# FNet and GeGLU on one Trainium2 core: an eighth pass of the sequence DFT as seven block products, with its preparations moved ahead

## The chip, the cores and the metric

The kernel runs on one core of a Trainium2 chip. Its engines work side by side, each on its own instructions in the order in which the program gives them: TensorE (PE) multiplies, VectorE (DVE) and ScalarE (ACT) work element by element, GpSimd (POOL) helps, and SyncE (SP) issues the transfers between the device's memory and the core. An instruction that waits holds up everything behind it on its own engine; this holds for SP's transfers too. The metric is the device time of one execution in microseconds (us), as the median of several runs.

## The reference

```python
def _A_ref(x, dft_seq_re, dft_seq_im, dft_hid_re, dft_hid_im):
    a = jnp.einsum("bsd,ed->bse", x, dft_hid_re)
    b = jnp.einsum("bsd,ed->bse", x, dft_hid_im)
    y = jnp.einsum("ts,bse->bte", dft_seq_re, a) - jnp.einsum("ts,bse->bte", dft_seq_im, b)
    return y

def _B_ref(x, w_gate, w_up, w_down):
    g = jnp.einsum("bsd,df->bsf", x, w_gate)
    u = jnp.einsum("bsd,df->bsf", x, w_up)
    h = _gelu(g) * u
    return jnp.einsum("bsf,fd->bsd", h, w_down)
...
h = x + _A_ref(_layernorm(x, axis=-1), A_dft_seq_re, A_dft_seq_im, A_dft_hid_re, A_dft_hid_im)
h2 = h + _B_ref(_layernorm(h, axis=-1), B_w_gate, B_w_up, B_w_down)
```

x has 2048 rows of 448 columns. It is normed, the real part of its Fourier transform over the sequence and over the hidden dimension is formed as two products with cosine and sine matrices, and x is added. The sum h is normed and goes through a feed-forward part: a gate and an up product (448 by 1792 each), GELU of the gate times the up part, and a down product back to 448 columns, added to h.

## The kernel before

**Number format.** Every operand of a product is split into two fp16 halves, *hi* (the rounded value) and *lo* (what rounding left), and a product is three terms: hi by hi, hi by lo, lo by hi. ACT makes hi (L108), DVE makes lo (L112 or L114) out of the fp32 value and hi; so each split is a hand-over from ACT to DVE.

**Stages.** First comes the sequence DFT, the product of the 2048 x 2048 cosine and sine matrices (parts 0 and 1) with the normed x; its output comes in eight groups of 256 rows, called p = 0 to 7, each of two halves g. Behind each p comes its hidden DFT (`hid_mm`, 21 matmuls for each g). Then follow the gate and up products and the down product; the profile's lines L1039 and L1243 are theirs.

**Steps.** The sequence DFT is written as 64 steps (`N_STEPS`). Steps 0 to 15 take the 16 tiles of x as they come and fill eight accumulators (p = 0 and 1); `x_load`, `x_stats`, `x_hi`, `x_lo` prepare tile n + 2 or n + 3 in step n. From step 16 on, a pass is four steps, and two passes (part 0, part 1) make one p. A normal step is 24 matmuls of 448 columns and needs one weight tile `wr` split into `ws`. From step `FAST` = 36 on, a pass is computed as seven block products instead of eight (Strassen's scheme): 42 matmuls of 224 columns a step. It needs sums of weight blocks, made for each step by `fast_sums` (DVE), `fast_raw` and `fast_split` (ACT hi, DVE lo), together called the unit of a step, and sums of x tiles, called T0 to T7, which are made once: `t_load` reads two x tiles again (`tx`), `t_norm` norms them on ACT, `t_sums` adds them in four DVE instructions, `t_hi` and `t_lo` split them. T j is used in the step of a pass with j = 2 (n mod 4) + i, so T6 and T7 in its last step. The result of a fast pass, `zs`, is also split into hi and lo.

**What sets the order.** The order is written out by hand. `early[n]` holds work that is issued at the start of step n, `after[(n, half)]` work that is issued behind the first or second half of step n's matmuls. What stands earlier in the program comes earlier on every engine that it uses.

**Work that is slotted in.** `Weights(f, k)` loads a chunk f of the gate and up weights into `gu_raw` (two DMAs), `sums` adds blocks of it on DVE, `split(True)` splits the raw blocks, `split(False)` splits the sums, one step after another. `gu_raw` shares two buffers with `wh_raw`, the raw tiles of the hidden DFT's matrix: a load into one waits until the tile before in that buffer has been split. The first chunks, 13 and 11, follow wh_raw1 and wh_raw2. `hid_seed` (ACT, L712) writes x into the accumulator of a hidden DFT, of which there is one for all, and `hid_out` (ACT, L720 to L722) reads it when `hid_mm` is done; the seed for g = 1 thus stands behind the reading of g = 0. The layernorm of the feed-forward part (`ffn_norm_act`, `ffn_sums`, `ffn_split`) is also spread over the steps. The rings have 3 buffers for x tiles, 5 for `wr`, 6 for `ws`, and 7 PSUM banks for sums of the sequence DFT.

```python
fast_at = [FAST + n for n in (-4, -2, -1)] + list(range(FAST + 1, N_STEPS - 2))
```

Of the kernel before, what the change touches and what calls it, by code (L numbers as in the profile page):

```python
# [32 lines left out]
def kernel(  # L33
# [76 lines left out]
    def lo_part(dst, src, hi, scale=1.0):  # L110
        if isinstance(scale, float) and scale == 1.0:
            V.tensor_sub(dst, src, hi)  # L112
        else:
            V.scalar_tensor_tensor(dst, src, scale, hi, op0=ALU.mult, op1=ALU.subtract)  # L114
# [301 lines left out]
    N_STEPS = NT + 8 * (NP - 2)  # L416
# [32 lines left out]

    FAST = N_STEPS - 28
    A_RAW = ("A12", "A11", "A22")
    FORMS = ("S3", "S1", "S2", "S4")
    T_OPS = ("T1", "T3", "T4", "T2")
    PRODUCTS = ("A11", "B11"), ("A12", "B21"), ("S2", "T2"), ("S3", "T3"), ("S1", "T1"), ("S4", "B22"), ("A22", "T4")
    fast_w, fast_s, fast_t, fast_acc, fast_e = {}, {}, {}, {}, {}

    def fast_views(n):
        raw = wr[n].rearrange("p (i b t) -> p i b t", i=2, b=4)  # L460
# [5 lines left out]
    def fast_sums(n):  # L466
        fast_s[n] = dft.tile([P, 8 * P], F32, tag="wr", bufs=5, name=f"sums{n}")
        fast_w[n] = [fast_tile(n, k, **place) for k, place in enumerate(fast_places(n))]
        raw, s, src, dst = fast_views(n)
        by_block = raw.rearrange("p i b t -> p b i t")  # L470
        V.tensor_add(s[:, 0:2], by_block[:, 1:3], by_block[:, 3:4].to_broadcast([P, 2, 2, P]))  # L471
        V.tensor_add(s[:, 2], s[:, 1], raw[:, :, 1])
        V.tensor_add(s[:, 3], raw[:, :, 0], s[:, 2])
# [56 lines left out]
    def fast_halves(n):  # L530
        p, part, qq = step_of(n)
        hi, lo = [zs[p][:, :, l, part * D : (part + 1) * D] for l in range(2)]
        src = fast_e[n][:, 0 : 2 * D].rearrange("p (g d) -> p g d", g=2)
        hi_part(hi, src)
        lo_part(lo, src, hi)

    def fast_out(n, k):

# [207 lines left out]


    gu, gw = {}, {}
    DFT_F = ((13, 14, 0), (11, 16, 1), (9, 18, 0), (7, 20, 1), (5, 22, 0), (3, 24, 1), (0, 28, 0), (1, 32, 0))
    JIT_F = range(2, 13, 2)  # L750

    early, after = {}, {}
# [10 lines left out]
        nc.sync.dma_start(gw[f], w_dram[f])  # L763

    for i, (f, n, k) in enumerate(DFT_F):
        ahead = 4 if i < 2 or n - DFT_F[i - 2][1] > 4 else 3
        at(after, (n - ahead, 0), lambda f=f, k=k: gu.update({f: Weights(f, k)}))
        at(early, n, lambda f=f: gu[f].sums())
        at(early, n + 1, lambda f=f: gu[f].split(True))
        at(early, n + 2, lambda f=f: gu[f].split(False))  # L770
        at(after, (n + 3, 0), lambda f=f: gu[f].store())
# [6 lines left out]
    for p, (n, half) in enumerate(turns):  # L778
        b, j = divmod(p, 2)
        m = (19, 24, 29, 36, 44, 52, 60)[p]  # L780
        last = ((20, 0), (25, 0), (30, 0), (38, 0), (48, 0), (56, 0), (61, 1))[p]
        m1 = last[0] + 1
        at(early, m - 4, lambda b=b, j=j: h_tile(b, j))
        at(early, m - 2, lambda p=p: hid_seed(p, 0))
        for g in range(2):

            place = last if g else (m, 0)
            at(after, place, lambda p=p, g=g: hid_mm(p, g), lambda p=p, g=g: hid_out(p, g))
            if g == 0:
                at(after, (m, 0), lambda p=p: hid_seed(p, 1))  # L790
        at(after, (n, half), lambda p=p: z_turn(p))
        at(early, m1 + p // 3 if p < 5 else N_STEPS - 7 + p, lambda b=b, j=j: ffn_rstd(b, j))
        at(after, (m1, 0), lambda b=b, j=j: h_store(b, j))
        if b < 2:

            m += 4 if p == 3 else 0
            at(early, m + 2, lambda b=b, j=j: ffn_bias(b, j), lambda b=b, j=j: ffn_norm_act(b, j, hp[b, j]))
            at(early, m + 3, lambda b=b, j=j: ffn_sums(b, j))
            at(early, m + 4, lambda b=b, j=j: ffn_split(b, j))
            for k in range(4):  # L800
                at(after, (m + 5 + k // 2, k % 2), lambda b=b, j=j, k=k: ffn_transpose(b, j, (k,)))
# [1 line left out]
    at(early, N_STEPS - 2, lambda: h_tile(NB - 1, 1))  # L803
    at(early, N_STEPS - 1, gelu_table)
    at(after, (N_STEPS - 2, 0), lambda: down_load(0), lambda: down_load(1))
    for j, n in ((0, 17), (1, 20), (4, 23), (5, 26), (6, 29), (2, 31), (3, 34), (7, 37)):
        at(after, (n - 2, 1), lambda j=j: t_load(j))
        at(early, n, lambda j=j: t_norm(j), lambda j=j: t_sums(j))
        at(after, (n, 0), lambda j=j: t_hi(j))
        at(after, (n, 1), lambda j=j: t_lo(j))  # L810
# [38 lines left out]
    for n in range(N_STEPS):  # L849
        if n == 0:  # L850
            for key in first:
                seq_acc(*key, last=key == first[-1])
        elif n >= FAST and n % 4 == 0:
            fast_begin(n)
        elif n >= NT and n % 4 == 0:
            for g in range(2):
                seq_acc(*step_of(n)[:2], g)
        if n + 3 < NT:
            x_load(n + 3)
        if n + 3 < FAST:  # L860
            seq_load(n + 5)

        if 0 < n < FAST - 3:
            seq_hi(n + 3)
        if 0 < n < NT - 2:
            x_rstd(n + 2)
            x_hi(n + 2)
            x_norm(n + 2)
        if 0 < n < NT - 3:
            x_stats(n + 3)  # L870
        if n == 0:
            seq_lo(2)
        if n + 3 < FAST:
            seq_lo(n + 3)
        if n in fast_at:
            unit = fast_at.index(n) + FAST
            fast_sums(unit)

            if n < FAST or n % 4 < 3:
                fast_raw(unit)  # L880
                fast_split(unit)
                if unit + 2 < N_STEPS:
                    seq_load(unit + 2)
        if n == 0:
            x_stats(3)
            x_lo(2)
        if 0 < n < NT - 2:
            x_lo(n + 2)
        for what in early.get(n, ()):
            what()  # L890
        if n >= FAST:

            last = n % 4 == 3
            one = [(i, k) for k in range(7) for i in range(2)] if last else [(i, k) for i in range(2) for k in range(7)]
            if n % 4 == 0 and n > FAST:

                one = [(i, k) for i in range(2) for k in range(5)] + [(i, k) for i in range(2) for k in (5, 6)]
            for m, (i, k) in enumerate(one):  # L900
                fast_mm(n, i, k)
                if last and i == 1 and k in (0, 2, 4, 6):
                    fast_out(n, k)
                    if n < N_STEPS - 1:
                        unit = n + 2
                        if k == 2:
                            fast_raw(unit)
                        elif k == 4:
                            fast_split(unit)
                            if unit + 2 < N_STEPS:  # L910
                                seq_load(unit + 2)
                if m in (6, 13):
                    for what in after.get((n, m // 7), ()):
                        what()
            continue

        if n < NT:
            one = [(key, n - n % 2 + key[0], 2 * (2 * key[1] + key[2]) + n % 2, n) for key in first]
            if n == 0:

                order = [(0, m) for m in (0, 2, 1)] + [(1, m) for m in range(3)]
                one = [(*a, (m,)) for jj, m in order for a in one[4 * jj : 4 * jj + 4]]
            elif n < 6:
                one = [(*a, (m,)) for m in (0, 2, 1) for a in one]
            else:
                one = [(*a, range(3)) for a in one]
        else:
            p, part, qq = step_of(n)
            one = [
                ((p, part, g), n, 4 * i + 2 * g + c, 4 * qq + 2 * i + c, range(3))  # L930
                for i in range(2)
                for g in range(2)
                for c in range(2)
            ]
            if qq == 3:

                one.sort(key=lambda a: a[0])
        for half in range(2):
            for key, unit, block, c, terms in one[half * len(one) // 2 : (half + 1) * len(one) // 2]:
                seq_mm(key, ws[unit], block, c, terms)  # L940
                if c == NT - 1 and 2 in terms and (n < NT or block in (5, 7)):
                    z_out(*key)
            for what in after.get((n, half), ()):
                what()
    z_turn(NP - 1)
    down_sums(0)
    gu[JIT_F[1]] = Weights(JIT_F[1], JIT_F[1] % 3)
# [331 lines left out]
    for q, t0, step, when in ((2, 5, 3, AT_A), (3, 14, 6, AT_B)):  # L1279
# [22 lines left out]
    right.close()  # L1302
    ps_ff = {
        tag: ctx.enter_context(tc.tile_pool(name=f"ps_{tag}", bufs=1, space=bass.MemoryType.PSUM, reuse_waits="tile"))
        for tag in ("Y", "X", "a0", "a1", "a2", "a3", "Z")
    }
    ps_ff["tr"] = ps_tr

# [11 lines left out]
    for t in range(NF):  # L1320
        w = gu.get(t + 2) if t + 2 in JIT_F else None
        n = PREP_AT.get(t)
# [258 lines left out]
```

## Time and profile before

| what | value |
|---|---|
| median of 3 runs | 701.72 us (701.16 to 701.92) |
| profiled execution, its own time | 701.11 us |
| its span | 699.3 us, 13800 instructions |
| PE busy | 694.1 us, 99% of the span |
| DVE busy | 556.3 us, 80% |
| ACT busy | 402.1 us, 57% |
| POOL busy | 106.7 us, 15% |
| granted TensorE clock | 1.00 |
| moved by DMA | 160.40 MB, mean 229 GB/s |

Busy time is counted in the profiled execution; its own time is longer than its span by 1.8 us, which lie around the span. The span starts with the first instruction. Rows of a timeline give start, duration, engine, line, operation, output and inputs by their names, shapes, a count, and in brackets the idle time before it with what ended it.

### The profile page before, as it was taken

How to read it: one execution, taken by the hardware profiler on the slowest of the kernel's cores; microseconds unless marked ns; L12 is line 12 of the kernel's file. 1: busy time of each engine (PE TensorE's matmuls, PEld its weight loads, DVE VectorE, ACT ScalarE, POOL GpSimd, SP SyncE). 2: the span in 40 equal slices, each digit the busy share in tenths (PEclk: the TensorE clock that was granted, in tenths of full speed). 3: DMA queues.
4: the chain of work that ended last, by engine and by line, in shares of the span. 5: the costliest groups of instructions: out<-in, count | busy, mean ns of one | idle time of the engine just before them, and what ended most of it. 6: DMA issues, size and time to landing. Idle time of an engine off the chain costs nothing.

```text
span 699.3 us, 13800 instructions
## 1 busy us (share of the span) xinstructions
PE 694.1 (99%) x5236; PEld 506.9 (72%) x5236; DVE 556.3 (80%) x1150; ACT 402.1 (57%) x789; POOL 106.7 (15%) x127
## 2 busy tenths in 40 slices
PE   8999999999999999999999999999999999999998
PEld 5555555555579888997644444469999999999997
DVE  7998766865899999985548798786777867899786
ACT  5877566675585556554427666655555453655631
POOL 0000000000001001000303333521120211232224
PEclk9999999999999999999999999999999999999999
DMA  8788888999876477374766878797879995877612
GB/s 276 244 238 284 242 290 215 328 279 294 221 216 166 122 196 199 124 210 174 148 226 230 284 241 251 191 334 234 216 227 331 243 302 174 321 277 273 231 42 80
DMA packets 116179, 160.40 MB, mean 229 GB/s; under 512 B 61968, under 2 KB 80528, under 8 KB 116112
## 3 DMA queue, kind: packets, MB, share of 16 engines
q1 hardware_dynamic: 116112, 159.51, 74.5%
q8 instruction: 41, 0.67, 0.4%
q14 instruction: 26, 0.21, 0.1%
HBM read 111.25 MB, written 34.34 MB: 208 GB/s over the span
## 4 chain that ended last, share of the span: by engine, by line
PE 94%; DVE 2%; ACT 2%; issue 1%; DMA 0%; POOL 0%; DVEq 0%; ACTq 0%; POOLq 0%
PE acc L645 20%; PE acc_f L521 16%; PE acc_d L1243 15%; PE pY L1039 15%; PE pZ L1039 10%; PE pX L1039 10%; PE y L731 9%; DVE gu_w L114 0%; ACT ws L108 0%; DMA x<-in_x_dram 0%; DVE ws L114 0%; DVE xs L112 0%; ACT y L722 0%; ACT hx L720 0%; ACT dn_w L108 0%
## 5 line engine op out<-in xcount | busy, mean ns | idle before, releaser
L1039 PEld LDWEIGHTS <-gw 128*128 128x128 f16 x1404 | 137.1, 98 | 47.0
L645 PE MATMUL acc<-xs,ws 128*128 128x448 f16 x864 | 164.7, 352 | 0.5 <-DVE xs L149 0.5
L645 PEld LDWEIGHTS <-ws 128*128 128x128 f16 x864 | 84.5, 98 | 79.5 <-ACT ws L108 0.6
L521 PEld LDWEIGHTS <-ws 128*128 128x128 f16 x1176 | 112.7, 98 | 1.6
L1243 PE MATMUL acc_d<-wd,dn_w 128*128 128x224 f16 x1008 | 110.6, 259 | 0.0
L1243 PEld LDWEIGHTS <-dn_w 128*128 128x128 f16 x1008 | 96.9, 98 | 1.9
L1133 POOL TENSOR_TENSOR hs<-hs,c 128x256 f32<-128x256 f32 (+1 forms) x42 | 59.8, 1423 | 247.9 <-ACT c L1131 182.0
L1039 PE MATMUL pY<-hops,gw 128*128 128x256 f16 (+1 forms) x612 | 94.2, 296 | 0.0
L114 DVE SCALAR_TENSOR_TENSOR ws<-wr,ws 128x1024 f16<-128x1024 f32 (+2 forms) x66 | 70.9, 1076 | 14.2 <-ACT ws L108 13.7
L521 PE MATMUL acc_f<-t,ws 128*128 128x224 f16 x672 | 80.4, 259 | 0.0
L731 PE MATMUL y<-wh,z 128*128 128x448 f16 x336 | 66.2, 352 | 0.1
L1039 PE MATMUL pZ<-hops,gw 128*128 128x256 f16 (+1 forms) x396 | 64.4, 296 | 0.0
L1039 PE MATMUL pX<-hops,gw 128*128 128x256 f16 (+1 forms) x396 | 64.4, 296 | 0.0
L521 PE MATMUL acc_f<-xs,ws 128*128 128x224 f16 x504 | 64.3, 259 | 0.0
L108 ACT ACTIVATE ws<-wr 128x1024 f16<-128x1024 f32 (+2 forms) x66 | 61.1, 927 | 4.5 <-DMA wr<-in_w_seq_dram 3.2
L1084 ACT ACTIVATE pY<-pX 128x256 f32<-128x256 f32 (+1 forms) x42 | 18.4, 439 | 66.9 <-PE pX L1039 66.5
L731 PEld LDWEIGHTS <-z 128*128 128x128 f16 x336 | 32.8, 98 | 29.6 <-issue 0.3
L1095 ACT ACTIVATE u<-pY 128x256 f32<-128x256 f32 (+1 forms) x42 | 19.1, 454 | 53.6 <-PE pY L1039 53.5
L1049 DVE SCALAR_TENSOR_TENSOR c<-pZ,u 128x256 f32<-128x256 f32 (+1 forms) x42 | 21.4, 510 | 35.4 <-PE pZ L1039 19.3
L108 ACT ACTIVATE ws<-sums 128x512 f16<-128x512 f32 x56 | 34.4, 626 | 24.3 <-DVE sums L471 19.4
L1039 PEld LDWEIGHTS <-gu_w 128*128 128x128 f16 x234 | 22.9, 98 | 27.6
L112 DVE TENSOR_TENSOR dn_w<-dn_s,dn_w 128x640 f16<-128x640 f32 x48 | 41.6, 868 | 1.5 <-ACT dn_w L108 1.4
(145 smaller groups left out, 931.9 us busy)
## 6 DMA issues: line engine op xcount, KB each, us to landing
gw<-w_dram SPq DMA_DIRECT2D x36, 896.0 KB, 6.2
wr<-in_w_seq_dram SPq DMA_DIRECT2D x100, 256.0 KB, 4.5
hid_dram<-hs SPq DMA_DIRECT2D x27, 512.0 KB, 5.7
hid<-hid_dram SPq DMA_DIRECT2D x54, 256.0 KB, 5.4
w_dram<-gu_w SPq DMA_DIRECT2D x14, 896.0 KB, 5.5
gu_raw<-in_w_gu_dram SPq DMA_DIRECT2D x28, 384.0 KB, 5.6
wr<-in_w_seq_dram SPq DMA_DIRECT2D x14, 512.0 KB, 5.2
x<-in_x_dram SPq DMA_DIRECT2D x16, 224.0 KB, 3.8
```

What stands on the lines that cost most here:

```text
L108: A.activation(dst, src, AF.Copy, scale=scale)
L112: V.tensor_sub(dst, src, hi)
L114: V.scalar_tensor_tensor(dst, src, scale, hi, op0=ALU.mult, op1=ALU.subtract)
L521: PE.matmul(fast_sum(n, k), fast_a(n, i, lw, a), fast_b(j, lx, b), start=j == 0 and m == 0 and k in (0, 1, 3, 5), stop=j == NT // 2 - 1 an ...
L645: PE.matmul(acc[key][:, :D], w[:, lw, block * P : (block + 1) * P], xs[c][:, lx, :], start=c == 0 and m == 0, stop=c == NT - 1 and m == 2,)
L731: PE.matmul(y[:, :D], z[p][:, lz, k, g * P : (g + 1) * P], wh[:, lw, k, :], start=p == NP - 1 and k == 0 and m == 0, stop=k == 6 and m == ...
L1039: PE.matmul(ps, w[:, wl, wa + ws, :], ops[:, m + ms, :], start=first and n == 0, stop=last and n == len(terms) - 1, skip_group_check=True,)
L1049: V.scalar_tensor_tensor(dst, ps, SC, other, op0=ALU.mult, op1=ALU.add)
L1084: A.activation(self.Y, self.X, AF.Copy)
L1095: A.activation(self.u2, self.Y, AF.Copy, scale=SC)
L1133: G.tensor_mul(c22, c22, self.cols(self.c12))
L1243: PE.matmul(ps, w[:, la, a, :], wd[n][:, lb, b, :], start=n == 0 and m == 0 and opens, stop=n == NC - 1 and m == 2, skip_group_check=True,)
```

## The change

- `FAST` goes from 36 to 32. One more pass (p = 4, part 0, steps 32 to 35) is computed as seven block products, and all units of weight sums begin four steps sooner, since `fast_at`, the list of steps in which the units are made, counts from `FAST`.
- The T sums are made sooner and in another order: T0 at step 15 (before 17), T1 at 18 (20), T6 at 20 (29), T2 at 28 (31), T3 at 31 (34), T7 at 33 (37); T4 and T5 stay.
- The weight chunks of the sequence part are summed and split two steps sooner (the last two four steps). With `ahead` 3 instead of 4 for the first two, their loads are issued one step sooner, behind the first half of steps 9 and 11.
- The low half of a fast pass's `zs` is no longer made at once but behind the DVE sums of the next unit.
- The feed-forward layernorm of p = 3 comes five steps later.
- The PSUM pools of the feed-forward part are opened in another order.

```diff
-    FAST = N_STEPS - 28
+    FAST = N_STEPS - 32
...
-    fast_w, fast_s, fast_t, fast_acc, fast_e = {}, {}, {}, {}, {}
+    fast_w, fast_s, fast_t, fast_acc, fast_e, last_lo = {}, {}, {}, {}, {}, []
...
         hi_part(hi, src)
-        lo_part(lo, src, hi)
+        last_lo.append(lambda: lo_part(lo, src, hi))
...
-    DFT_F = ((13, 14, 0), (11, 16, 1), (9, 18, 0), (7, 20, 1), (5, 22, 0), (3, 24, 1), (0, 28, 0), (1, 32, 0))
+    DFT_F = ((13, 12, 0), (11, 14, 1), (9, 16, 0), (7, 18, 1), (5, 20, 0), (3, 22, 1), (0, 24, 0), (1, 28, 0))
...
-        ahead = 4 if i < 2 or n - DFT_F[i - 2][1] > 4 else 3
+        ahead = 4 if i > 1 and n - DFT_F[i - 2][1] > 4 else 3
         at(after, (n - ahead, 0), lambda f=f, k=k: gu.update({f: Weights(f, k)}))
...
-            m += 4 if p == 3 else 0
+            m += 9 if p == 3 else 0
...
-    for j, n in ((0, 17), (1, 20), (4, 23), (5, 26), (6, 29), (2, 31), (3, 34), (7, 37)):
+    for j, n in ((0, 15), (1, 18), (6, 20), (4, 23), (5, 26), (2, 28), (3, 31), (7, 33)):
...
             fast_sums(unit)
+            while last_lo:
+                last_lo.pop()()
...
+    last_lo.pop()()
     z_turn(NP - 1)
...
-        for tag in ("Y", "X", "a0", "a1", "a2", "a3", "Z")
+        for tag in ("a0", "a1", "a2", "a3", "Z", "Y", "X")
```

Three places show how this moves instructions. Names with a number behind the underscore are tiles; `x13` is the 14th tile of x, `gu_raw13` chunk 13 of the gate and up weights.

The first is SP's queue in steps 9 to 13. Before:

```order
L371 DMA x13_734<-in_x_dram 128x448
L427 DMA wr15_736<-in_w_seq_dram 128x1024
L323 DMA gu_raw13_769<-in_w_gu_dram 128x768 x2
L371 DMA x14_784<-in_x_dram 128x448
L432 DMA wr16_786<-in_w_seq_dram 128x512 x2
L371 DMA x15_834<-in_x_dram 128x448
L432 DMA wr17_836<-in_w_seq_dram 128x512 x2
L323 DMA gu_raw11_870<-in_w_gu_dram 128x768 x2
```

And after:

```order
L323 DMA gu_raw13_722<-in_w_gu_dram 128x768 x2
L371 DMA x13_737<-in_x_dram 128x448
L427 DMA wr15_739<-in_w_seq_dram 128x1024
L371 DMA x14_784<-in_x_dram 128x448
L432 DMA wr16_786<-in_w_seq_dram 128x512 x2
L323 DMA gu_raw11_822<-in_w_gu_dram 128x768 x2
L371 DMA x15_837<-in_x_dram 128x448
L432 DMA wr17_839<-in_w_seq_dram 128x512 x2
```

The loads of chunk 13 and chunk 11 now stand ahead of x13 and x15; before, they stood behind them.

The second is DVE between the lo of x15 (`xs15`) and the first two lo parts of `zs0`, which empty the first accumulators. Before:

```order
L112 TENSOR_TENSOR xs15_893<-x15_834,xs15_893 128x448
L114 SCALAR_TENSOR_TENSOR ws17_926<-wr17_836,ws17_926 128x1024
L328 TENSOR_TENSOR gu_s13_929<-gu_raw13_769 128x384
L329 TENSOR_TENSOR gu_s13_929<-gu_s13_929,gu_raw13_769 128x384
L330 TENSOR_TENSOR gu_s13_929<-gu_raw13_769 128x256
L331 TENSOR_TENSOR gu_s13_929<-gu_raw13_769,gu_s13_929 128x256
L114 SCALAR_TENSOR_TENSOR ws18_961<-wr18_885,ws18_961 128x1024
L114 SCALAR_TENSOR_TENSOR gu_w13_964<-gu_raw13_769,gu_w13_964 128x512
L114 SCALAR_TENSOR_TENSOR gu_w13_964<-gu_raw13_769,gu_w13_964 128x256
L114 SCALAR_TENSOR_TENSOR zs0_171<-acc0_00_249,zs0_171 128x448
```

And after, from the split of `ws17` on:

```order
L114 SCALAR_TENSOR_TENSOR ws17_943<-wr17_839,ws17_943 128x1024
L114 SCALAR_TENSOR_TENSOR gu_w13_904<-gu_s13_861,gu_w13_904 128x512 x2
L328 TENSOR_TENSOR gu_s11_950<-gu_raw11_822 128x384
L329 TENSOR_TENSOR gu_s11_950<-gu_s11_950,gu_raw11_822 128x384
L330 TENSOR_TENSOR gu_s11_950<-gu_raw11_822 128x256
L331 TENSOR_TENSOR gu_s11_950<-gu_raw11_822,gu_s11_950 128x256
L114 SCALAR_TENSOR_TENSOR ws18_982<-wr18_890,ws18_982 128x1024
L114 SCALAR_TENSOR_TENSOR gu_w11_985<-gu_raw11_822,gu_w11_985 128x512
L114 SCALAR_TENSOR_TENSOR gu_w11_985<-gu_raw11_822,gu_w11_985 128x256
L579 TENSOR_TENSOR tx0_0_936<-tx0_0_936 128x224
L580 TENSOR_TENSOR tx0_0_936<-tx0_1_937,tx0_0_936 128x224
L581 TENSOR_TENSOR tx0_1_937<-tx0_0_936,tx0_1_937 128x224
```

The split of chunk 13's sums, sums and raw split of chunk 11 and the four sums of T0 (the fourth, L582, and then `zs0` come next) have moved ahead of `zs0`; the sums and raw split of chunk 13 stand further ahead still.

The third is ACT around step 29, where `y_2_0` and `y_2_1` are the hidden DFT's accumulator for p = 2, g = 0 and g = 1. Before:

```order
L393 ACTIVATE tx6_0_1728<-tx6_0_1728,affine_166 128x448
L393 ACTIVATE tx6_1_1729<-tx6_1_1729,affine_166 128x448
L720 ACTIVATE hx1_0_1567,mv_h1_0_1834<-y_2_0_1696 128x448
L721 ACTIVATE mv_h1_0_1834<-mv_h1_0_1834 128x1
L722 ACTIVATE y_2_0_1696,mv_h1_0_1834<-y_2_0_1696,mv_h1_0_1834 128x448
L712 ACTIVATE y_2_1_1838<-hx1_0_1567 128x448
L108 ACTIVATE t6_1840<-tx6_0_1728 128x448
L108 ACTIVATE t6_1840<-tx6_1_1729 128x448
```

And after:

```order
L393 ACTIVATE tx2_0_1716<-tx2_0_1716,affine_166 128x448
L393 ACTIVATE tx2_1_1717<-tx2_1_1717,affine_166 128x448
L108 ACTIVATE t2_3_1821<-tx2_0_1716 128x448
L108 ACTIVATE t2_3_1821<-tx2_1_1717 128x448
L108 ACTIVATE gu_w1_1838<-gu_raw1_1541 128x512
L108 ACTIVATE gu_w1_1838<-gu_raw1_1541 128x256
L720 ACTIVATE hx1_0_1600,mv_h1_0_1877<-y_2_0_1733 128x448
L721 ACTIVATE mv_h1_0_1877<-mv_h1_0_1877 128x1
L722 ACTIVATE y_2_0_1733,mv_h1_0_1877<-y_2_0_1733,mv_h1_0_1877 128x448
L712 ACTIVATE y_2_1_1881<-hx1_0_1600 128x448
```

The hi parts of a T, which need that T's sums from DVE, have moved from behind the seed of `y_2_1` to ahead of the reading of `y_2_0`, and the raw split of chunk 1 stands there too.

## The prediction

> **What bounds the kernel now.** I read the page's busy times and its chain first, then the chain of waits in order of time for the length of a step, and last the timelines of SP, DVE and ACT where the change moves work.
>
> ```profile
> PE 694.1 (99%) x5236; PEld 506.9 (72%) x5236; DVE 556.3 (80%) x1150; ACT 402.1 (57%) x789; POOL 106.7 (15%) x127
> PE 94%; DVE 2%; ACT 2%; issue 1%; DMA 0%; POOL 0%; DVEq 0%; ACTq 0%; POOLq 0%
> ```
>
> TensorE works 99% of the span and carries 94% of the chain. Fewer matmuls shorten the kernel only as long as TensorE never waits; and there is almost no wait left to win. DVE at 80% is next.
>
> ```profile
> 39.97 54.67 PE acc L645 x289
> 138.02 18.16 PE acc L645 x96
> 164.53 4.14 PE L731 MATMUL y<-wh,z 128*128 128x448 f16 x21
> 300.01 16.10 PE acc_f L521 x168
> ```
>
> The first row is steps 8 to the middle of step 19 without a wait: 54.67 / 289 = 0.189 us a matmul, 4.54 a step of 24. It ends at 94.64, three and a half steps (84 matmuls) after step 16 began, so step 16 began at 78.75 and step 14 at 69.67. These are the dates that new work on the other engines has to meet. The third row is the hidden DFT of p = 2, g = 1, in step 30.
>
> **The gain (A).** A normal pass is 96 matmuls in 18.16, a fast one 168 in 16.10 (4.03 a step, 0.096 a matmul). One pass less: **-2.06**. Everything else can only be free or cost.
>
> **The front (B).** First SP's queue, where the loads of chunks 13 and 11 now stand ahead of x13 and x15.
>
> ```profile
> 47.23 0.33 SPq L371 DMA_DIRECT2D x<-in_x_dram  x1
> 51.70 0.81 SPq L323 DMA_DIRECT2D gu_raw<-in_w_gu_dram  x2
> 52.55 0.43 SPq L371 DMA_DIRECT2D x<-in_x_dram  x1
> 55.05 0.33 SPq L371 DMA_DIRECT2D x<-in_x_dram  x1
> 60.31 1.28 SPq L323 DMA_DIRECT2D gu_raw<-in_w_gu_dram  x2
> ```
>
> The x rows are x13, x14, x15, the others chunk 13 and chunk 11. DVE at the same time:
>
> ```profile
> 51.06 0.62 DVE L114 SCALAR_TENSOR_TENSOR wh<-wh_raw,wh 128x448 f16<-128x448 f32 x1
> 52.31 0.62 DVE L122 BATCH_NORM_STATS2 st_x<-x 128x6 f32<-128x448 f32 x1
> 56.56 0.63 DVE L122 BATCH_NORM_STATS2 st_x<-x 128x6 f32<-128x448 f32 x1 [0.82 <-DMA x<-in_x_dram]
> 59.19 1.09 DVE L114 SCALAR_TENSOR_TENSOR wh<-wh_raw,wh 128x896 f16<-128x896 f32 x1
> 60.91 0.62 DVE L122 BATCH_NORM_STATS2 st_x<-x 128x6 f32<-128x448 f32 x1
> 63.01 0.62 DVE L112 TENSOR_TENSOR xs<-x,xs 128x448 f16<-128x448 f32 x1
> ```
>
> Chunk 13's load waits for the buffer of wh_raw1, whose split ends at 51.68; SP goes on at 51.70. Chunk 11 waits for wh_raw2 in the same way (split until 60.28, load at 60.31). So x13 is no longer issued at 47.23 but behind chunk 13, at 52.55, where x14 was. x14 landed 4.0 later, at 56.56, and its statistics had to wait for it; so x13's statistics now start at 56.56 instead of 52.31. From there DVE's order is the old one: from x13's statistics to x14's 4.25 less the idle 0.82, 3.43; from x14's to the end of the next wh split 60.2 - 56.56 = 3.6: the split of wh_raw2 ends about 63.6. Only then chunk 11's load leaves (1.28), then x15 at 64.9, which by the same 4.0 lands at 68.9. Its statistics come at 68.9 instead of 60.91, and x14's lo part, which stood 2.63 behind them (63.54), ends at 71.5. TensorE needs it for the second matmul of step 14, 69.86. First wait: **1.7**.
>
> DVE then still has to do what now stands ahead of the first zs:
>
> ```profile
> 66.91 1.22 DVE L114 SCALAR_TENSOR_TENSOR ws<-wr,ws 128x1024 f16<-128x1024 f32 x1 [0.32 <-ACT ws L108]
> 68.05 0.55 DVE L328 TENSOR_TENSOR gu_s<-gu_raw 128x384 f32<-128x384 f32 x1
> 70.92 1.02 DVE L114 SCALAR_TENSOR_TENSOR gu_w<-gu_raw,gu_w 128x512 f16<-128x512 f32 x2
> 75.39 4.60 DVE L114 SCALAR_TENSOR_TENSOR zs<-acc,zs 128x448 f16<-128x448 f32 x8 [3.45 <-ACT zs L108]
> 81.45 1.28 DVE L114 SCALAR_TENSOR_TENSOR gu_w<-gu_s,gu_w 128x512 f16<-128x512 f32 x2
> 86.58 0.39 DVE L579 TENSOR_TENSOR tx<-tx 128x224 f32<-128x224 f32 x1
> 88.24 0.62 DVE L112 TENSOR_TENSOR t<-tx,t 128x448 f16<-128x448 f32 x1
> ```
>
> A split of ws is 1.14 (66.91 to 68.05); a chunk's sums are 70.92 - 68.05 less one such split, 1.73; its raw split is 0.93, its sums' split 1.3; the sums of a T 88.24 - 86.58 = 1.66. From x14's lo: x15 and ws16 3.0 (63.54 to 66.59), sums of two chunks 3.46, two raw splits 1.9, one sums' split 1.3, ws17 and ws18 2.3, T0's sums 1.66, together 13.6: zs begins at 85.1, its first lo is done at 85.7, with hand-overs 86.0. Before, DVE stood idle 3.45 until 75.39 and began as soon as the accumulators were full. TensorE needs the first accumulators empty for step 16, 78.75. So the two waits are together 7.3. **B = +7.3**, from 5.5 (if hand-overs vanish and x15 lands 1.5 sooner, as no row excludes) to 8.5 (T0's two tiles are loaded behind chunk 9, whose buffer comes free about 77; they land around 82.4 and are normed by 83.5, no later than DVE comes to them).
>
> **Steps 28 to 30 (C).** The new fast pass needs unit 32 in step 28, and T2 is made there. ACT reads the hidden DFT of p = 2, g = 0 (`hid_out`) and writes the seed of g = 1 only behind T2's hi and chunk 1's raw hi; before, T6's hi stood behind the seed.
>
> ```profile
> 147.79 1.08 SPq L432 DMA_DIRECT2D wr<-in_w_seq_dram  x2
> 149.39 1.23 SPq L432 DMA_DIRECT2D wr<-in_w_seq_dram  x2
> 153.06 1.06 ACT L108 ACTIVATE ws<-wr 128x1024 f16<-128x1024 f32 x1 [1.46 <-DMA wr<-in_w_seq_dram]
> 155.29 0.55 DVE L328 TENSOR_TENSOR gu_s<-gu_raw 128x384 f32<-128x384 f32 x1
> 157.03 0.42 DVE L112 TENSOR_TENSOR xs<-xn_h,xs 128x256 f16<-128x256 f32 x1
> 159.10 1.22 DVE L114 SCALAR_TENSOR_TENSOR ws<-wr,ws 128x1024 f16<-128x1024 f32 x1
> 225.40 0.67 DVE L471 TENSOR_TENSOR sums<-wr 128x512 f32<-128x512 f32 x1
> 228.91 0.69 DVE L471 TENSOR_TENSOR sums<-wr 128x512 f32<-128x512 f32 x1
> 160.25 0.54 ACT L720 ACTIVATE hx<-y 128x448 f32<-128x448 f32 x1 [0.72 <-PE y L731]
> 161.91 0.55 ACT L712 ACTIVATE y<-hx 128x448 f32<-128x448 f32 x1
> ```
>
> A weight load issued at 147.79 lands at 153.06, 5.3 later. wr32's load, 149.39 before, now stands behind T2's two tiles (about 1.1) and lands at 155.8; DVE is free at 155.29. From 155.8, on before's clock: unit 32 is 3.52 (228.91 - 225.40), chunk 1's sums 1.74 (155.29 to 157.03), the layernorm's lo 2.07 (157.03 to 159.10), T2's sums 1.66: 164.8. Then ACT: T2's last hi 0.5 (448 columns, as the row at 160.25), the raw hi 0.85 (768 columns in two pieces, from 1.06 for 1024 in the row at 153.06), hid_out 1.66 (160.25 to 161.91), the seed 0.55: 168.4. TensorE wants to begin at 164.53. **C = +3.9**. Below, 1.5, if B's delay lets DVE enter step 28 early; above, 5, if ACT's own splits of unit 32 are also in the way.
>
> **Step 35 (D).** T7 is used first by the sixth group of three matmuls in step 35.
>
> ```profile
> 168.77 0.54 ACT L720 ACTIVATE hx<-y 128x448 f32<-128x448 f32 x1 [3.26 <-PE y L731]
> 179.77 1.15 DVE L112 TENSOR_TENSOR t<-tx,t 128x448 f16<-128x448 f32 x2
> 187.24 0.42 DVE L254 TENSOR_TENSOR tt<-xn_h 128x256 f32<-128x256 f32 x1
> 188.71 1.02 DVE L114 SCALAR_TENSOR_TENSOR gu_w<-gu_raw,gu_w 128x512 f16<-128x512 f32 x2
> ```
>
> Call the end of the hidden DFT of step 30 E (168.5 before). ACT reads it at 168.77, and the layernorm behind it feeds DVE. The T of step 31 was done at 180.84, E + 12.3; with a unit's hi parts (0.9) instead of a tile's on ACT it is E + 13.1. Behind it DVE has the layernorm's sums 1.47 (187.24 to 188.71), unit 35 3.52, the layernorm's lo 2.07, T7 2.9 (1.66 and twice 0.62): E + 23.1. TensorE comes to it 2.27 (half a step 30), 4.54, three steps of 4.03 and five groups of 0.29 after E: E + 20.4. **D = +2.7**, from 0 (T6's 2.9 of DVE are gone from step 29, which may give all of it back) to 4; step 36's units, behind T7, +0.2.
>
> **Edits at no cost.** The postponed lo part takes away DVE's wait for ACT's hi, once a pass; if that cover fails, the next pass's bank waits at most the 0.6 of the lo. The five steps for p = 3's layernorm move DVE work from units 45 to 47 to units 50 and 51; if DVE has no lead there, each step pays its share of the 3.5. The other chunks change places with their like. The PSUM order changes no bank that TensorE asks for first.
>
> **Sum.** -2.06 + 7.3 + 3.9 + 2.7 + 0.2 = +12.0 on the profiled execution's 701.11, of which 699.3 is span: 713.1. The median of the runs shown is 0.61 above it, 701.72, so I forecast **713.8**.
>
> **Rivals.**
> - *Absorbed (the other side).* DVE's added work vanishes in its idle time; the row at 75.39 alone shows 3.45 of it, and the 63.01 row ends 6.3 before TensorE needs its tile. Were the loads of x13 and x15 not held up, B would be 13.6 from 63.5: zs at 77.1, before 78.75. Then 701.72 - 2.06 = 699.7. It is decided by whether zs's first lo comes before 78.75. Against it: SP is in order, and 51.70 and 60.31 follow a DVE split by 0.03.
> - *Only one place pays.* B alone gives 707.0, C and D alone 706.5. A late TensorE gives DVE time, so the later waits may shrink.
> - *The clock.* The start shows what a pause costs:
>
> ```profile
> 1.36 4.00 PE L102 MATMUL pw<-ident 128*128 128x128 f16 x44 [1.36 <-POOL sign_t L93]
> ```
>
> 44 matmuls in 4.00 are 91 ns for 128 columns; at 0.189 for 448, 128 columns are 54 ns. After an idle stretch TensorE thus begins at 0.6 of its pace, and 4 us of it lose 1.6 us. If the waits of B's second part and C, both above 3.4, do this once each, the time is 713.8 + 3.3 = 717.1. For it: that row. Against it: it is the only such row, and no wait in the middle of before is long.
>
> The Trainium skill ("TensorE: Matmul & The Clock Gate", section "What's actually happening") says that the clock falls to half after an idle window of about 3.4 us and comes back after as long a busy one. By that rule, two such pauses would cost about 1.7 each and the time would be 717.2; the row of the start agrees in kind, no row here shows it in the middle of a kernel.
>
> **Chances.** Absorbed 0.08; no change 0.03; one place alone 0.22; all three 0.52; all three and the clock 0.15. The range reaches from the one-place cases (706) to the clock (718). Faster by over 0.2% (1.4 us, about what these runs can tell from none) 0.08, within 0.03, slower 0.89.
>
> **What would show it.** Right: x13's statistics on DVE move by some 4 us behind chunk 13's load; a TensorE idle time of 1 to 2 at step 14 and 5 to 6 at step 16, ended by DVE's zs or ACT behind it; one of 3 to 4 ahead of the hidden DFT in step 30, ended by ACT's seed; one of 2 to 3 in step 35, ended by T7; four steps of 4.03 from step 32. Wrong: x13 landing in time because SP is not held up, or DVE idle ahead of zs as before; then B falls, and with it most of the sum.

## The result and the profile after

The changed kernel takes 718.75 us (median of 6 runs, 717.70 to 722.41), the kernel before 701.38 (6 runs). The ratio is 1.0257, with an interval of 1.0231 to 1.0283: 17.4 us slower, where 12.0 were forecast, and above the range, which ended at 718. The profiled execution is the slowest of the six, 722.41; its waits and its clock are read below with that in mind.

The page after, busy times and the chain by engine:

```profile
PE 699.3 (97%) x5308; PEld 516.3 (72%) x5308; DVE 567.5 (79%) x1169; ACT 404.9 (56%) x797; POOL 106.3 (15%) x127
PE 76%; DVE 10%; DMA 5%; ACT 3%; issue 2%; SPq 2%; POOL 0%; DVEq 0%; ACTq 0%; POOLq 0%
```

TensorE carried 94% of the chain and carries 76% now; DVE, DMA and SP's queue have come into it. TensorE is busy 5.2 longer, though its matmuls are 2.06 us less work: some ran slowly. Who TensorE waited for, after (us in total, times, longest):

```profile
PE y L731 <- ACT y L712: 6.0, 1, 6.0
PE acc L645 <- DVE zs L114: 5.4, 1, 5.4
PE acc L645 <- DVE xs L112: 2.7, 1, 2.7
PE acc_f L521 <- ACT t L108: 2.2, 1, 2.2
...
PE acc_f L521 <- DVE t L112: 0.4, 1, 0.4
```

These are the four places of the prediction: step 30 (seed), step 16 (zs), step 14 (x14's lo), step 35 (T7, two rows). By the rows of TensorE's timeline they are 6.02, 5.36, 2.65 and 2.22 + 0.39, in all 16.6.

**The front.** SP's queue after:

```profile
52.59 0.81 SPq L323 DMA_DIRECT2D gu_raw<-in_w_gu_dram  x2
53.45 0.43 SPq L371 DMA_DIRECT2D x<-in_x_dram  x1
...
64.93 0.81 SPq L323 DMA_DIRECT2D gu_raw<-in_w_gu_dram  x2
65.79 0.43 SPq L371 DMA_DIRECT2D x<-in_x_dram  x1
```

x13 now leaves at 53.45 behind chunk 13, x15 at 65.79 behind chunk 11. DVE after:

```profile
57.73 0.63 DVE L122 BATCH_NORM_STATS2 st_x<-x 128x6 f32<-128x448 f32 x1 [4.45 <-DMA x<-in_x_dram]
...
69.63 0.63 DVE L122 BATCH_NORM_STATS2 st_x<-x 128x6 f32<-128x448 f32 x1 [4.00 <-DMA x<-in_x_dram]
...
71.73 0.62 DVE L112 TENSOR_TENSOR xs<-x,xs 128x448 f16<-128x448 f32 x1
72.26 0.55 DVE L328 TENSOR_TENSOR gu_s<-gu_raw 128x384 f32<-128x384 f32 x1
...
86.30 3.81 DVE L114 SCALAR_TENSOR_TENSOR zs<-acc,zs 128x448 f16<-128x448 f32 x7
```

The statistics of x13 and x15 wait 4.45 and 4.00 for their tiles. DVE goes on from x14's lo at 72.26 (forecast 71.5), zs begins at 86.30 (forecast 85.1), with no idle time ahead of it.

**Step 30.** The same on SP, DVE, ACT and TensorE:

```profile
161.77 1.25 SPq L432 DMA_DIRECT2D wr<-in_w_seq_dram  x2
168.02 0.69 DVE L471 TENSOR_TENSOR sums<-wr 128x512 f32<-128x512 f32 x1 [1.92 <-DMA wr<-in_w_seq_dram]
178.50 0.52 ACT L720 ACTIVATE hx<-y 128x448 f32<-128x448 f32 x1
180.74 6.91 PE L731 MATMUL y<-wh,z 128*128 128x448 f16 x21 [6.02 <-ACT y L712]
```

Unit 32 begins when wr32 lands, 6.25 after its load was issued; ACT reads `y_2_0` at 178.50, TensorE waits 6.02. And then 21 matmuls take 6.91, where they took 4.14.

**Step 35.** T7 on DVE and TensorE:

```profile
200.67 0.42 DVE L254 TENSOR_TENSOR tt<-xn_h 128x256 f32<-128x256 f32 x1
207.74 0.38 DVE L579 TENSOR_TENSOR tx<-tx 128x224 f32<-128x224 f32 x1
210.85 2.77 PE L521 MATMUL acc_f<-t,ws 128*128 128x224 f16 x14 [0.39 <-DVE t L112]
```

**The clock.** Stretches of the changed kernel: length, PE busy (matmuls), granted clock, DMA share, GB/s. 1.00 is the full clock. The first pair lies around step 16's wait, the second around step 30's, the last three around step 35's. Ahead of them stand TensorE's rows for the matmuls behind step 14's wait and step 16's.

```profile
72.40 9.21 PE L645 MATMUL acc<-xs,ws 128*128 128x448 f16 x47 [2.65 <-DVE xs L112]
86.97 17.94 PE L645 MATMUL acc<-xs,ws 128*128 128x448 f16 x84 [5.36 <-DVE zs L114]
...
80.00:87.00 7.00, 1.64 (x10) 0.79 0.97 321
87.00:92.00 5.00, 5.00 (x17) 0.62 1.03 416
...
173.00:181.00 8.00, 1.98 (x11) 0.91 0.62 147
181.00:187.00 6.00, 6.00 (x19) 0.55 1.08 276
...
209.00:210.00 1.00, 0.00 (x0) 1.00 0.72 186
211.00:212.00 1.00, 1.00 (x7) 0.50 0.98 368
214.00:215.00 1.00, 1.00 (x13) 1.00 1.18 81
```

Behind the waits of steps 16, 30 and 35 TensorE works at half its clock: 7 matmuls a microsecond instead of 13 behind step 35's, for some 3 us. Behind step 14's wait of 2.65 it doesn't: 47 matmuls take 9.21, 0.196 each, at a clock of 1.00. In this execution the 84 matmuls behind step 16's wait take 17.9 instead of 15.9, step 30's hidden DFT 2.8 too long, the 14 in step 35 some 1.3: 6.1 together. Then 701.11 - 2.06 + 16.6 + 6.1 = 721.8 of the 722.41. The six runs differ in this: two had a mean clock of 0.988 and took 721.1 and 722.4, four had 0.992 or 0.993 and took 717.7 to 719.2. The difference of the clocks, 0.0048 of 718, is some 3.4 us, that of the times 3.7. With the same waits, 701.38 - 2.06 + 16.6 leave 2.8 for the clock in the median; this is a remainder, since no trace shows the median run.

### The profile page after: what moved, and what is told of

The parts are those of the page before. It is cut to its first block, busy times and chain, and to the rows that moved or that the text cites. A ratio compares the mean times of both kernels' runs of the same rounds, so it can differ in the third digit from the quotient of the medians.

```text
span 720.5 us, 13983 instructions
## 1 busy us (share of the span) xinstructions
PE 699.3 (97%) x5308; PEld 516.3 (72%) x5308; DVE 567.5 (79%) x1169; ACT 404.9 (56%) x797; POOL 106.3 (15%) x127
## 4 chain that ended last, share of the span: by engine, by line
PE 76%; DVE 10%; DMA 5%; ACT 3%; issue 2%; SPq 2%; POOL 0%; DVEq 0%; ACTq 0%; POOLq 0%
PE acc_f L521 17%; PE acc_d L1246 15%; PE pY L1042 14%; PE pX L1042 9%; PE pZ L1042 9%; PE y L731 8%; PE acc L645 4%; DMA wr<-in_w_seq_dram 3%; DVE ws L114 2%; DMA x<-in_x_dram 2%; DVE xs L112 2%; DVE st_x L122 1%; DVE gu_w L114 1%; SPq L670 1%; ACT ws L108 1%
## 5 line engine op out<-in xcount | busy, mean ns | idle before, releaser
L645 PE MATMUL acc<-xs,ws 128*128 128x448 f16 x768 | 148.8, 355 | 8.0 <-DVE zs L114 5.4
L521 PEld LDWEIGHTS <-ws 128*128 128x128 f16 x1344 | 129.6, 98 | 5.2 <-issue 2.9
L645 PEld LDWEIGHTS <-ws 128*128 128x128 f16 x768 | 75.6, 99 | 79.9 <-issue 11.0
L521 PE MATMUL acc_f<-t,ws 128*128 128x224 f16 x768 | 93.5, 261 | 2.6 <-ACT t L108 2.2
L114 DVE SCALAR_TENSOR_TENSOR ws<-wr,ws 128x768 f16<-128x768 f32 (+2 forms) x66 | 69.9, 1060 | 15.7 <-ACT ws L108 15.7
L731 PE MATMUL y<-wh,z 128*128 128x448 f16 x336 | 69.0, 363 | 6.0 <-ACT y L712 6.0
L521 PE MATMUL acc_f<-xs,ws 128*128 128x224 f16 x576 | 73.6, 259 | 0.0
L108 ACT ACTIVATE ws<-wr 128x768 f16<-128x768 f32 (+2 forms) x66 | 60.6, 918 | 14.2 <-DMA wr<-in_w_seq_dram 8.4
L1098 ACT ACTIVATE u<-pY 128x256 f32<-128x256 f32 (+1 forms) x42 | 19.1, 455 | 53.8 <-PE pY L1042 53.7
L108 ACT ACTIVATE ws<-sums 128x512 f16<-128x512 f32 x64 | 37.7, 620 | 12.7 <-DVE sums L471 9.9
L204 POOL TENSOR_SCALAR r_h<-mv_h 128x2 f32<-128x2 f32 x7 | 1.5, 212 | 281.2 <-ACT y L722 281.2
```

The costliest lines, as they stand in the source:

```text
L108: A.activation(dst, src, AF.Copy, scale=scale)
L521: PE.matmul(fast_sum(n, k), fast_a(n, i, lw, a), fast_b(j, lx, b), start=j == 0 and m == 0 and k in (0, 1, 3, 5), stop=j == NT // 2 - 1 an ...
L645: PE.matmul(acc[key][:, :D], w[:, lw, block * P : (block + 1) * P], xs[c][:, lx, :], start=c == 0 and m == 0, stop=c == NT - 1 and m == 2,)
L731: PE.matmul(y[:, :D], z[p][:, lz, k, g * P : (g + 1) * P], wh[:, lw, k, :], start=p == NP - 1 and k == 0 and m == 0, stop=k == 6 and m == ...
L1098: A.activation(self.u2, self.Y, AF.Copy, scale=SC)
```

## The experiments

The theory: four waits made by order, each independent of the others, and a slow clock behind the longer ones. The rivals: the amount of added DVE work as such; waits that come back elsewhere; slow matmuls for another reason.

**Front, both directions.** First the loads back where they were, in the changed kernel:

```diff
-        ahead = 4 if i > 1 and n - DFT_F[i - 2][1] > 4 else 3
+        ahead = 2 if i < 2 else 4 if n - DFT_F[i - 2][1] > 4 else 3
```

> The changed kernel, with the loads of chunks 13 and 11 issued one step later again, behind x13 and x15 as before the change; DVE's order stays that of the change. Theory (the loads of x behind a buffer's release make the front wait): x13 and x15 land as before, x14's lo part ends near 63.5, then 13.6 us of DVE bring the first zs lo to about 78 to 79, against 78.75: the waits of 2.65 and 5.36 us at steps 14 and 16 go down to 0 to 0.5 together, and with them the slow clock behind the second; time about 709.5 (708 to 711). Rival (the amount of DVE work ahead of zs makes it wait, whatever the loads): the wait at step 14 goes, 4 to 5 us stay at step 16, time about 715.

Measured 709.53 (709.04 to 710.87). TensorE's waits and DVE's zs:

```profile
PE y L731 <- ACT y L712: 5.0, 1, 5.0
PE acc_f L521 <- ACT t L108: 2.2, 1, 2.2
```

```profile
77.39 4.33 DVE L114 SCALAR_TENSOR_TENSOR zs<-acc,zs 128x448 f16<-128x448 f32 x8
```

Both front waits are gone, with all of the moved DVE work still ahead of zs: it begins at 77.39, in time for 78.75, and the time lies where the theory put it. The loads' places alone turn DVE's idle time into a wait. Then the loads one step sooner in the kernel before, and nothing else:

```diff
-        ahead = 4 if i < 2 or n - DFT_F[i - 2][1] > 4 else 3
+        ahead = 5 if i < 2 else 4 if n - DFT_F[i - 2][1] > 4 else 3
```

> The kernel before, with the loads of chunks 13 and 11 one step sooner (SP's order there as in the changed kernel) and nothing else. Theory (late x tiles and the work moved ahead of zs each use up the same slack, so their costs don't simply add): x14's lo ends about 72, the wait at step 14 is 1.7 to 2.7, then DVE has 8.4 us of its old work up to zs, whose first lo ends about 81, against TensorE at 80.4 to 81.4: 0 to 0.6 there; time 703 to 704.8. Rival (the loads alone make all of the front's 8.0 us): 709 or more. Rival (x13 and x15 land in time anyway): 701.4.

Measured 703.03 (701.95 to 707.68), ratio 1.0036 (1.0018 to 1.0055).

```profile
68.70 0.63 DVE L122 BATCH_NORM_STATS2 st_x<-x 128x6 f32<-128x448 f32 x1 [3.97 <-DMA x<-in_x_dram]
...
79.65 4.33 DVE L114 SCALAR_TENSOR_TENSOR zs<-acc,zs 128x448 f16<-128x448 f32 x8
```

x15 is nearly as late here (68.70 against 69.63), zs begins at 79.65, and TensorE waits only 1.76 at step 14 and not at step 16. So the loads alone cost 2, the work alone nothing, and both together 8: they draw on one slack.

**Step 30.** T2 one step later:

```diff
-    ... (5, 26), (2, 28), (3, 31), (7, 33)):
+    ... (5, 26), (2, 29), (3, 31), (7, 33)):
```

> The changed kernel, with T2 made in step 29 instead of 28, so that its hi parts stand behind hid_out and the seed of step 29 on ACT. Theory (T2's hi ahead of hid_out holds up the seed): the wait of 6.02 us ahead of the hidden DFT of step 30 and the slow clock behind it go; time about 711 (709.5 to 712.5), waits at steps 14, 16 and 35 as they were (2.6, 5.4, 2.6 us). Rival (unit 32, whose weights land late, holds up ACT with or without T2): 3 us or more of the wait stay, time about 715.

Measured 714.54 (713.82 to 715.78).

```profile
PE acc L645 <- DVE zs L114: 5.3, 1, 5.3
PE acc_f L521 <- ACT t L108: 2.4, 1, 2.4
PE acc_f L521 <- DVE t L112: 1.7, 2, 1.4
...
PE acc L645 <- DVE xs L112: 1.3, 1, 1.3
```

The wait ahead of the hidden DFT is gone, which speaks against the rival; but T2 is now late for step 33 (1.4), and only 4.2 of the expected 7.7 came back. In the profiled executions the waits fell from 16.6 to 10.8 together, which is more than the medians show; why the median fell by less stays open. With the loads back as well (the edit of the first experiment and this one):

> Both edits together. Theory (the waits are independent of each other): gain -2.06, front about +0.3, step 30 about 0, step 35 +2.6 and some slow clock behind it: about 702.5 (701.5 to 704). Rival (a wait removed early comes back later, since DVE has the same work in less time): step 30 or step 35 waits 3 us more than in the changed kernel, time 705 or more.

Measured 705.38 (704.42 to 706.12), above the 704 at which the expectation ended. The waits left in the profile are 0.87 at step 33 and 2.82 at step 35, and behind the second the clock was 0.50 for some 3.4 us, which loses 1.7. Neither the front's nor step 30's wait came back when the other was gone: the two are independent. Step 33's wait is the part of the rival that holds, 0.9 instead of 3.

**Step 35.** Both edits, and the layernorm of p = 2 four steps later:

```diff
-            m += 9 if p == 3 else 0
+            m += 9 if p == 3 else 4 if p == 2 else 0
```

> Both edits, and the feed-forward layernorm of p = 2 four steps later (as the change does for p = 3 by five), so that T3 and T7 no longer stand behind the layernorm's statistics and its DVE work. Theory (step 35's wait is T7 behind that layernorm): the wait of 2.6 us at step 35 goes, time about 699.7 (699 to 701), faster than before by the gain of the pass. Rival (DVE has no room in steps 36 to 40 for the 3.5 us of the layernorm): the wait moves to steps 36 to 41, time about 702.

Measured 699.38 (7 runs, 698.95 to 700.84), ratio 0.9972 (0.9961 to 0.9984): faster than the kernel before, by about the gain of the pass. The waits at steps 33 and 35 are gone, and with no wait above a microsecond behind the start the clock is full:

```profile
0.00:200.00 200.00, 197.16 (x1161) 1.00 0.90 264
200.00:400.00 200.00, 200.00 (x1590) 1.00 0.67 188
```

Two waits of 0.82 and 0.66 for seeds remained in its profile, which is of the longest of the seven runs (700.84). T4 one step later, and then chunk 1 too, were to take them away:

```diff
-    ... (6, 20), (4, 23), (5, 26), ...
+    ... (6, 20), (4, 24), (5, 26), ...
```

> The kernel of e5_ffn_later (699.38) with T4 made in step 24 instead of 23, so that its hi parts stand behind hid_out of step 24. Theory (the same mechanism as in step 30, at a smaller size): the wait of 0.82 us ahead of the hidden DFT of step 25 goes, time about 698.6. Rival (T4 then delays T5 and what is behind it by as much): no change, 699.4.

```diff
-    DFT_F = (... (0, 24, 0), (1, 28, 0))
+    DFT_F = (... (0, 24, 0), (1, 29, 0))
```

> The kernel of e7_t4_behind with chunk 1's sums and splits one step later (29 instead of 28), so that its raw hi parts (0.92 us of ACT) stand behind hid_out of step 29. Theory: the wait of 0.66 us ahead of the hidden DFT of step 30 goes too, time about 698.0. Rival (DVE's sums of chunk 1 then delay T2 and unit 33, which step 33 waits for): a wait of 0.5 to 1.5 at step 33, time 698.6 to 700.

T4: 699.77 (698.99 to 700.95), its interval overlaps that of the kernel without it, and no gain can be measured. Both waits are gone from the profile, but they are also missing in that of the version below with a low half made at once, where T4 stands in its old place; so they vary between executions, and it isn't shown that T4's move took them away. Chunk 1: 702.85 (701.30 to 703.71), 3 slower instead of faster. The seed's wait that was to go is in the profile (0.9), and there are four waits for `ws` from step 36 on, 1.6 together: the rival's cause, in later steps than it said. DVE has no lead left there.

**The edits costed at nothing**, in the kernel before, with `last_lo` as in the change, and:

```diff
-            m += 4 if p == 3 else 0
+            m += 9 if p == 3 else 0
...
-        for tag in ("Y", "X", "a0", "a1", "a2", "a3", "Z")
+        for tag in ("a0", "a1", "a2", "a3", "Z", "Y", "X")
```

> The kernel before, with only the three edits that the prediction costed at nothing: the low half of a fast pass's result behind the next sums, the layernorm of p = 3 five steps later, the other PSUM order. Theory (all hidden): the time of the kernel before within 0.2%, 700.2 to 702.6, with no TensorE wait over 0.5 us. Rival (the moved 3.5 us of DVE work meets steps 48 to 51 without a lead, or the first gate and up products wait for a bank): a new wait of 0.5 to 2 us there, time 702 to 703.5.

And one of them undone in the fastest version:

```diff
-        last_lo.append(lambda: lo_part(lo, src, hi))
+        lo_part(lo, src, hi)
```

> The kernel of e5_ffn_later (699.38), with the low half of a fast pass's result made at once again, ahead of the next sums. Theory (as the prediction has it, DVE's wait of 1.0 us a pass is covered): 699.4, within 0.7. Rival (with eight fast passes and three things moved later DVE has no lead left in steps 36 to 48): TensorE waits 0.3 to 1 us in some of the passes, 700.5 to 703.

In the kernel before 701.32, ratio 0.9999 (0.9990 to 1.0008): nothing. The undone one 700.15, ratio 0.9991 (0.9982 to 1.0000), against 0.9972 with it: the intervals still touch. Its profile has two waits for `ws`, 0.5 together, that the other has not. It may be worth some tenths once eight passes leave DVE no lead; that isn't shown.

**The clock by itself.** Matmuls that nobody reads, put into the waits of the version with the loads back:

```diff
+    def keep_busy(count):
+        if not junk:
+            junk.append(ps_seq.tile([P, 512], F32, tag="mm", name="junk"))
+        for _ in range(count):
+            PE.matmul(junk[0][:, :D], xs[0][:, 0, 0:P], xs[1][:, 0, :], start=True, stop=True)
...
+        if (p, g) == (2, 1):
+            keep_busy(24)
...
+                if (n, i, k) == (35, 1, 2):
+                    keep_busy(10)
```

> The kernel of e1_loads_back (709.53) with matmuls that nobody reads put into its two waits: 24 (4.5 us) ahead of the hidden DFT of step 30, which waits 5.0 us there, and 10 (1.9 us) ahead of T7's first use in step 35, which waits 2.6. The waits end when they ended before. Theory (a paused TensorE starts again at half the clock): the hidden DFT takes 4.0 us instead of 6.1, time down by 2 to 3 to about 707 (706.3 to 707.7). Rival (the slower matmuls come from waiting for operands that trickle in, or cost nothing in the end): time as e1's, 709 to 710.5, or longer by what the extra matmuls take beyond the wait.

Measured 709.69 (708.21 to 713.63): inconclusive. In its profile, of the slowest run, the wait ended 2.65 later than in the version without, so that 2.22 of it were idle all the same; behind those the clock was 0.50 and the hidden DFT took 5.79. The runs with a mean clock of 0.999 or more took 708.2 to 710.7. So pauses were measured alone, in the kernel before:

```diff
+    def pause(count):
+        y = ps_tr.tile([P, 512], F32, tag="tr", name="y_held")
+        PE.matmul(y[:, :64], xs[0][:, 0, 0:P], xs[1][:, 0, 0:64], start=True, stop=True)
+        A.activation(held, y[:, :64], AF.Copy, scale=1e-12)
+        for _ in range(count):
+            G.tensor_mul(held, held, held)
+        hi_part(held_h, held)
+        PE.matmul(y[:, :64], xs[0][:, 0, 0:P], held_h, start=True, stop=True)
```

> The kernel before, with three short pauses of TensorE at the start of steps 40, 49 and 57: a small matmul, ACT copies its result, GpSimd multiplies the copy with itself twice, ACT rounds it, and a second small matmul reads that, which nobody uses. By the small rows of the trace (0.2 to 0.5 us each) a pause is 1.5 to 2.5 us. Theory (a pause of that length seldom starts the slow clock): time of before + the sum of the pauses, which the profile shows, + 0 to 1. Rival (any pause over some 1 us starts it): + 1.7 more for each pause, 5 in all.

> The same with nine multiplications in each pause, 4 to 6 us long. Theory (a pause of 4 us or more always starts TensorE at half the clock for 3 to 4 us): time of before + the sum of the pauses + 1.7 to 3 for each, 5 to 9 in all; matmuls of 224 columns at twice their time behind each pause. Rival (the slow matmuls behind the waits of the changed kernel had another cause, such as operands coming late): + 0, matmuls at their usual pace.

With two multiplications 728.05 (726.38 to 728.79), with nine 735.42 (735.04 to 735.83), kernel before 701.05. The pauses came out longer than estimated (the first of each kernel most):

```profile
228.08 0.21 PE L735 MATMUL y_held<-held_h,xs 128*128 128x64 f16 x1 [10.54 <-ACT held_h L108]
279.55 0.21 PE L735 MATMUL y_held<-held_h,xs 128*128 128x64 f16 x1 [4.30 <-ACT held_h L108]
326.64 0.21 PE L735 MATMUL y_held<-held_h,xs 128*128 128x64 f16 x1 [4.25 <-ACT held_h L108]
```

That is the first kernel, 19.1 in all; the second has 13.14, 7.07 and 7.01, 27.2 in all. In these two executions the span beyond that of before (699.3) and beyond the pauses is 726.9 - 699.3 - 19.1 = 8.5 and 733.2 - 699.3 - 27.2 = 6.7. The second kernel's stretches at its second pause show why:

```profile
277.44:284.51 7.07, 0.00 (x1) 0.87 1.00 192
284.51:286.00 1.49, 1.49 (x9) 0.50 0.99 394
286.00:287.00 1.00, 1.00 (x8) 0.50 0.70 268
...
289.00:290.00 1.00, 1.00 (x10) 0.75 0.00 0
290.00:291.00 1.00, 1.00 (x13) 1.00 0.00 0
```

Over the pause the clock is 0.87 in the mean, so it falls late in it; it is 0.50 when the matmuls come back, and full again only some 5 us later. The six stretches of half clock behind the pauses are 5.4, 5.1 and 5.8 us long in the first kernel, 3.9, 5.0 and 3.0 in the second. Half of that is lost, 8.2 and 5.9 of the 8.5 and 6.7. The theory's price (1.7 to 3) about holds: 1.5 to 2.9 for each pause of 4 us or more, 2.35 in the mean. Against the rival, operands coming late: TensorE waits for nothing behind the pauses in these profiles, and its matmuls are slow for just as long as the granted clock is 0.50. The short pause wasn't reached by these kernels; the waits of the others bear on it, below.

## Why the prediction was wrong

- **A, the gain: right.** 2.06 forecast. The version without the long waits is 0.9972 of before, 2.0 us (1.1 to 2.7 by its interval).
- **B, the front: right in its mechanism and nearly in its size**: 2.65 + 5.36 = 8.0 against 7.3, within its bounds; x14's lo came 0.8 later than worked out, and with the loads alone DVE went on from it at 71.34 against 71.5. Part of the size is luck: in the version with T2 later, whose order is the same up to there, the two waits were 1.32 and 5.30, 6.6 in all. The rival's arithmetic for loads that aren't held up (zs at 77.1) was met at 77.39.
- **C, step 30: the mis-sized term.** 6.0 against 3.9, and above its bound of 5, though not by what that bound was for (ACT's splits of unit 32). The chain from unit 32 to the seed was right: from 168.02 to 180.7 are 12.7, worked out 12.6. Its start was wrong: wr32 was taken to land 5.3 after its issue and took 6.25, and was issued later than the 1.1 of T2's loads. In the version with the loads back it landed at 157.06 instead of 155.8, and the wait was 5.03.
- **D, step 35: right.** From E = 187.65, an end on DVE taken as the start of its next row as in the prediction: T3 done at 200.67, E + 13.0 (13.1); T7's end 210.72, E + 23.1 (23.1); the wait 2.6 (2.7, and 0.2 for step 36 that didn't come).
- **Sum of the waits:** 16.6 against 14.1, 2.5 short.
- **The clock: the step that failed.** The prediction priced it (3.3 for two pauses) but gave it a chance of 0.15 and left it out of the sum, with the argument that the row of the start was the only one of its kind. No wait in the middle of before was long, so the kernel before could say nothing against it; forecast waits of 5 and 4 us called for it. It was 6.1 in the profiled execution and about 2.8 in the median. The median lies 5.0 above the forecast: 2.8 by the clock, 2.5 by the waits (C 2.1, B 0.7, step 35 and 36 less 0.3), less 0.3 because before measured 701.38 here and not 701.72. The forecast's own case with the clock, 717.1, still had C at 3.9; without the clock's 2.8, or without C's missing 2.1, the median would have been 715.9 or 716.6. The Trainium skill ("TensorE: Matmul & The Clock Gate", section "What's actually happening") says the same of the mechanism: half the clock after an idle window of about 3.4 us, back after a busy one. The traces agree in the half (0.50) and in pauses of 4 us or more; they differ in the shorter ones: of six waits of 2.2 to 2.8 us four were followed by it, below.
- **The zero-cost edits: right** for the kernel before (0.9999). The side of the sign was right, and *absorbed* turned out to be three edits away: it needs the loads of chunks 13 and 11 behind x13 and x15, T2 behind the reading of `y_2_0`, and p = 2's layernorm out of T7's way.

## What to carry to other kernels

Work that fits into an engine's idle time by its amount may still not fit by its place: what stands ahead of it in an in-order queue, here a load that waits for a buffer, decides. Where a change makes TensorE wait for several us, put the slow clock behind the wait into the sum, and not only among the rivals: in this kernel it came after every wait of over 4 us, and after some from 2.2 us on. When several waits are forecast, undo the order at each one separately: three such edits turned +17 us into -2.

## What the runs showed of the hardware

- Every pause of TensorE of 4.2 us or more in these profiles (the six of the last experiment, and the waits of 5.0 to 6.0 us at steps 16 and 30 of the changed kernel and two of its versions) was followed by 2.7 to 5.8 us at a clock of 0.50. Half of that is lost, 1.4 to 2.9 us beyond the pause.
- Within these ten pauses the clock fell 2.1 to 5.2 us after TensorE had stopped. This is an estimate from the mean clock over each pause, taken as full up to the fall and half behind it: 7.07 us at 0.87 are 1.84 at half, so the fall came after 5.2.
- Shorter ones are sometimes followed by it, too. Of waits of 2.2 to 2.8 us, three of step 35 (2.6 to 2.8, each with a single matmul inside) were followed by a clock of 0.50 and a fourth of 2.6 wasn't, one of 2.22 at step 30 was, and one of 2.65 at step 14 wasn't; none of 1.8 or less was, behind the start. In one of step 35's the clock fell only after work had begun again:

```profile
189.90:192.40 2.50, 0.08 (x2) 1.00 0.87 211
192.40:193.00 0.60, 0.25 (x1) 1.00 1.00 372
193.00:194.00 1.00, 0.95 (x10) 1.00 1.00 366
194.00:195.00 1.00, 1.00 (x8) 0.50 1.93 160
```

This is step 35 of the version with both edits: TensorE had been back for a microsecond, and 4 us had passed since it stopped. Such falls may be what makes runs of one kernel differ by several us, as the six of the changed kernel did; only their mean clocks speak for it. The waits fit the 2.1 to 5.2 us of the long pauses, but what sets that time in a given wait stays open.
